# A fused attention and gated-MLP kernel: row tiles issued from two queues, a weight block moved to ScalarE's queue, and the second chunk's statistics moved behind gate work

## The chip, the cores and the metric

The kernel runs on one core of a Trainium2 chip. The metric is the device time of one execution in microseconds (us), the median over several runs. The span that the profile shows is about 1.8 us shorter than the device time of the same run. Each run also lists the mean clock that TensorE (PE) was granted. That turns out to matter here: a stretch of 3.41 us at half clock lowers the mean over 280 us by 0.006, so a run at 0.994 had about one such stretch and a run at 0.988 had two.

## The reference, cut to what matters

```python
xn = layernorm(x)                       # x: 2048 x 640, bf16
qkv = xn @ wqkv                         # 32 heads of 20
pq, pk = q @ w_phi, k @ w_phi           # per head
phi = concat(softmax(p), softmax(-p))   # for q and for k
o = (phi_q @ (phi_k^T v)) / (phi_q @ sum(phi_k))
mlp = (silu(xn @ w1) * (xn @ w3)) @ w2  # 640 -> 1536 -> 640
out = x + o @ wo + mlp
```

## The kernel before

The 2048 rows are worked in four chunks of 512 rows, each of four row tiles of 128. Chunk 0 is normalised tile by tile (statistics on VectorE, DVE; square root on ScalarE, ACT), turned by TensorE (PE) transposes and used at once. Chunks 1 to 3 go through DRAM and a DMA transpose. PE's order is fixed: transposes T(0), T(1), then V(0), T(2), V(1), T(3), V(2), V(3), three gate/up (GU) pairs, the matmuls that fold `w_phi` into the key weights ("prep") with two more pairs, then K(0). Each engine gets its instructions in one fixed order, and where it matters below it keeps to it (in the profile of after_fill DVE stands idle for 3.75 us at one instruction with ready work behind it). All loads are issued from SyncE's queue:

```python
def setup():
    ...
    for t in range(4):
        load_x(xg[0], t, 1, 0)              # row tiles of chunk 0, 160 KB each
    nc.sync.dma_start(out=wv[:], ...)       # 800 KB
    load_gu(0)                              # 1st gate/up block: w1 and w3, 480 KB each
    nc.sync.dma_start(out=wrow[:], ...)
    load_x(xg[1], 0, 4, 1)                  # rows of chunk 1, 640 KB
    nc.sync.dma_start_transpose(out=wkT[:], in_=A_wqkv[:, D : 2 * D])
    for i in range(1, 4):
        load_gu(i)
...
    for t in range(4, 8):
        ln_stats(t)                         # statistics of chunk 1: on DVE ahead of all gate work
...
LN(1)                                       # normalise chunk 1, store it, transpose it back
```

A GU pair needs two PSUM banks of six. ACT takes tanh of one (`th`), DVE multiplies (`gs`), ACT copies the other (`up`), and only then are the banks free.

The softmax here doesn't subtract the row's maximum and nothing guards it: scores larger than these inputs give would overflow.

Of the kernel before, what the change touches and what calls it, by code (L numbers as in the profile page):

```python
# [79 lines left out]
def kernel(  # L80
# [53 lines left out]
    xg = {}  # L134
# [17 lines left out]
    wqkv3 = A_wqkv.rearrange("(c p) f -> p c f", p=P)  # L152
    w13 = [w.rearrange("(c p) f -> p c f", p=P) for w in (B_w1, B_w3)]

    def load_x(dst, t0, n, k):
        nc.sync.dma_start(
            out=dst[:, t0 : t0 + n, :],
            in_=x2[512 * k + t0 * P : 512 * k + (t0 + n) * P, :].rearrange("(t p) d -> p t d", p=P),
        )

    def load_gu(i):
        for w, src in zip((w1, w3), w13):
            nc.sync.dma_start(out=w[:, :, 384 * i : 384 * i + 384], in_=src[:, :, 384 * i : 384 * i + 384])

    def setup():
        xg[0] = five.tile([P, 4, D], bf, name="xg", tag="five")
        xn[0] = five.tile([P, 4, D], bf, name="xn", tag="five")
        xg[1] = five.tile([P, 4, D], bf, name="xg", tag="five")
        for t in range(4):
            load_x(xg[0], t, 1, 0)  # L170
        nc.sync.dma_start(out=wv[:], in_=wqkv3[:, :, 2 * D : 3 * D])
        load_gu(0)
        nc.sync.dma_start(out=wrow[:], in_=A_w_phi.rearrange("h j f -> (h j) f").rearrange("(g p) f -> p g f", p=P))
        load_x(xg[1], 0, 4, 1)
        nc.sync.dma_start_transpose(out=wkT[:], in_=A_wqkv[:, D : 2 * D])
        for i in range(1, 4):
            load_gu(i)

    ident = consts.tile([P, P], bf, name="ident")
    eps = consts.tile([P, 1], f32, name="eps")  # L180
# [21 lines left out]
    def warm():  # L202
        nc.vector.memset(xnT[:, 0, 0:512], 0.0)
        ps = bank([P, 512], f32)
        for i in range(WARM):
            nc.tensor.matmul(ps[:], xnT[:, 0, 0:P], xnT[:, 0, 0:512])
# [35 lines left out]
                nc.gpsimd.tensor_copy(out=hi[:, :, HC - 1], in_=mask[64:128, 2 * g + 1, :])  # L242

    pinned = {}

    def order_after(ins, other):
        tc.add_manual_dep(
# [12 lines left out]
    def dve_us(n, x=1):  # L260
        return 0.065 + n / 960.0 / x
# [1 line left out]
    stats = consts.tile([P, NST, 2, nc.vector.BN_STATS_DIM], f32, name="stats")  # L263
    mv = consts.tile([P, NST, nc.vector.BN_AGGR_DIM], f32, name="mv")
    rstd = consts.tile([P, NST], f32, name="rstd")
    arrive = [3.0, 4.4, 5.8, 6.2] + [11.0] * 4 
    stats_of = {}
    apply_of = {}
    rstd_of = {}
# [7 lines left out]
    def ln_stats(t, k=None, parts=(0, 1)):  # L277
        c, i = divmod(t, 4)

        def fn():  # L280
            for h in parts:
                ins = nc.vector.bn_stats(out=stats[:, t, h, :], in_=xg[c][:, i, h * 320 : (h + 1) * 320])  # L282
                if k is not None:
                    order_after(ins, pinned[k])
            if parts[-1] == 1:
                nc.vector.bn_aggr(out=mv[:, t, :], in_=stats[:, t, :, :])

        stats_of[t] = plan.op(
            "DVE", 0.47 * len(parts), fn, after=arrive[t] if t < 8 else 0.0,
            deps=[X_of.get(t)] + (phik_of[k][:1] if k is not None else []),  # L290
        )
        return stats_of[t]

# [43 lines left out]
    def LN(c, k=None):  # L337
        ln_rstd(c)

        def al():  # L340
            xn[c] = five.tile([P, 4, D], bf, name="xn", tag="five")

        a = xn_of[c] = plan.alloc("five", al)
        ds = [ln_apply(4 * c + i, [a] + (phik_of[k][:1] if k is not None else []), k) for i in range(4)]
        st = plan.op(
            "SP", 0.5,
            lambda: nc.sync.dma_start(out=xn_d[c][:].rearrange("(t p) d -> p t d", p=P), in_=xn[c][:]),
            deps=ds, frees=[a], lat=3.5,
        )
        xt = plan.op(  # L350
            "SP", 0.5,
            lambda: nc.sync.dma_start_transpose(out=xnT[:, :, 512 * c : 512 * c + 512], in_=xn_d[c][:]),
            deps=[st], lat=5.0,
        )
        for t in range(4 * c, 4 * c + 4):
            XT_of[t] = xt
# [66 lines left out]
    def K(t):  # L423
# [52 lines left out]
            plan.op("POOL", 1.7, mul(1), deps=[r2, pkb], frees=[ekb]),  # L476
        ]

    def KV(t):
        def fn():  # L480
            for j in range(10):
                acc = (kva, kvb)[j % 2]
                nc.tensor.matmul(  # L483
                    acc[:, 84 * (j // 2) : 84 * (j // 2) + 84],
                    phik_b[t][:, j, :, :].rearrange("p a f -> p (a f)"),
                    vaug[t % 4][:, h0[j] : h0[j] + 4, :].rearrange("p h d -> p (h d)"),
                    start=(t == 0 and j < 2), stop=(t == NST - 1), skip_group_check=True,
                )

        KV_of[t] = plan.op("PE", pe_us(10, 90), fn, deps=phik_of[t] + V_of[t], frees=[phik_a[t]])  # L490
# [39 lines left out]
    def hT_alloc(c):  # L530
        def fn():
            hT[c] = hpool.tile([P, KF, 512], bf, name="hT", tag="hT")

        if c not in hT_a:
            hT_a[c] = plan.alloc("hT", fn)
        return hT_a[c]

    w13_at = [10.0, 18.5, 21.5, 24.5]

    def GU(c, fi, mode):  # L540
        xs = xnT[:, :, c * 512 : (c + 1) * 512]
        deps = [XT_of[4 * c + i] for i in range(4)]
        us = []
        for w in (w1, w3):
            o = {}

            def fn(o=o, w=w):
                o["ps"] = bank([P, 512], f32)
                for k in range(KD):
                    nc.tensor.matmul(  # L550
                        o["ps"][:], w[:, k, fi * P : (fi + 1) * P], xs[:, k, :], start=(k == 0), stop=(k == KD - 1)
                    )

            us.append((plan.op("PE", pe_us(KD, 512), fn, deps=deps, takes="bank", after=w13_at[fi // 3]), o))
        (ug, og), (uu, ou) = us
        box = {}

        ab = {}
        for n in ("th", "gs") if mode == "DVE" else ("th", "gs", "up"):
            def al(n=n):  # L560
                box[n] = work.tile([P, 512], bf, name=n, tag=n)

            ab[n] = plan.alloc(n, al)

        def th():
            nc.scalar.activation(out=box["th"][:], in_=og["ps"][:], func=AF.Tanh, scale=0.5)  # L566

        a = plan.op("ACT", act_us(512), th, deps=[ug, ab["th"]], frees=[ug])

        def gs():  # L570
            nc.vector.scalar_tensor_tensor(  # L571
                out=box["gs"][:], in0=box["th"][:], scalar=1.0, in1=og["ps"][:], op0=ALU.add, op1=ALU.mult
            )

        b = plan.op("DVE", dve_us(512), gs, deps=[a, ab["gs"]], frees=[ug, ab["th"]])
        hb = hT_alloc(c)
        if mode == "DVE":

            def hm():
                nc.vector.scalar_tensor_tensor(  # L580
                    out=hT[c][:, fi, :], in0=box["gs"][:], scalar=0.5, in1=ou["ps"][:], op0=ALU.mult, op1=ALU.mult
                )

            d = plan.op("DVE", dve_us(512), hm, deps=[b, uu, hb], frees=[uu, ab["gs"]])
        else:

            def uc():
                nc.scalar.activation(out=box["up"][:], in_=ou["ps"][:], func=AF.Copy, scale=0.5)  # L588

            e = plan.op("ACT", act_us(512), uc, deps=[uu, ab["up"]], frees=[uu])  # L590
            d = plan.op(
                "POOL", 1.3,
                lambda: nc.gpsimd.tensor_mul(out=hT[c][:, fi, :], in0=box["gs"][:], in1=box["up"][:]),  # L593
                deps=[b, e, hb], frees=[ab["gs"], ab["up"]],
            )
        GU_of.setdefault(c, []).append(d)
# [244 lines left out]
    ln_finish(2)  # L841
    ln_stats(3, parts=(1,))
    ln_sqrt(3)
    V(0)
    T(2, "DVE")
    V(1)
    ln_finish(3)
    T(3, "DVE")
    V(2)
    V(3)  # L850
    plan.op("ACT", 1.3, lambda: nc.scalar.preload_act_table(AF.Exp), deps=[rstd_of[3]])

    for t in range(4, 8):
        ln_stats(t)
    early = len(plan.ops)

    plan.op("SP", 0.5, lambda: nc.sync.dma_start_transpose(out=wqT[:], in_=A_wqkv[:, 0:D]), after=24.0)
    LN(1)
    plan.op("SP", 0.5, lambda: nc.sync.dma_start(out=w2[:], in_=B_w2.rearrange("(c p) d -> p c d", p=P)), after=36.0)

    def modes(n):
# [15 lines left out]
            owed = 0.0  # L877

    fill(3 * 2.16)
    for u in prep("k", wkT, wkphi, 13.0):  # L880
        u()
        fill(0.4)
    wq_seq = prep("q", wqT, wqphi, 34.0)
    for t in range(NST):
        K(t)
        if 1 <= t <= 8:
            fetch(7 + t, t)
        if t == 5 or t == 9:
            LN((t + 3) // 4, t)
        fill(1.95)  # L890
        if t >= 4:
            V(t)
        fill(1.95)
        if t >= 2:
            KV(t - 2)
        if 6 <= t < 11:
            for _ in range(2):
                wq_seq.pop(0)()
                fill(0.4)
# [46 lines left out]

    order = plan.run()
    with tc.manual_schedule(engines={ET.PE, ET.DVE, ET.Activation, ET.Pool, ET.SP}):
        warm()
        setup()  # L950
        constants()
        for o in plan.ops[:early]:
            o["fn"]()
# [35 lines left out]
```

## Time and profile before

| | before |
|---|---|
| median of the first 6 runs | 280.86 us |
| PE busy | 271.1 of 279.4 us |
| first V matmul, first gate/up matmul, K(0) | 8.92, 16.57, 29.49 us |

The head of the page of before (engine, busy us, share, instructions) says that PE is the limit:

```profile
span 279.4 us, 4902 instructions
PE 271.1 (97%) x1880; PEld 166.1 (59%) x1904; DVE 172.3 (62%) x284; ACT 147.1 (53%) x320; POOL 95.7 (34%) x124
```

PE's timeline of before, first 17 us (start, duration, engine, line, operation, what ended the idle time ahead). V (line 401) waits for `wv` and then runs at half speed: 10 matmuls take 2.01 and 2.49 us, while 20 take 2.88 us from 13.86 us on.

```profile
5.92 0.67 PE L379 MATMUL bank<-ident,xn 128*128 128x128 bf16 x5
7.03 0.45 PE L379 MATMUL bank<-ident,xn 128*128 128x128 bf16 x5 [0.43 <-DVE xn L327]
8.92 2.01 PE L401 MATMUL bank<-wv,xnT 128*128 128x320 bf16 x10 [1.44 <-DMA wv<-in_A_wqkv_dram]
11.26 2.49 PE L401 MATMUL bank<-wv,xnT 128*128 128x320 bf16 x10
13.86 2.88 PE L401 MATMUL bank<-wv,xnT 128*128 128x320 bf16 x20
16.57 1.24 PE L550 MATMUL bank<-xnT,w_99 128*128 128x512 bf16 x4
```

The windows view of before (window: length, busy us of PE, PEld, DVE, ACT, POOL, granted clock, DMA share, GB/s). The windows are cut where the clock records begin and end. In 6.38 to 9.80 us PE worked 1.54 of 3.42 us; the next 3.41 us ran at half clock.

```profile
6.38:9.80 3.42, 1.54 (x15) 1.03 (x14) 2.74 (x9) 1.86 (x5) 3.01 (x17) 1.00 1.08 351
9.80:13.21 3.41, 3.41 (x18) 2.17 (x17) 1.01 (x3) 1.23 (x3) 2.32 (x9) 0.50 1.28 260
```

The chain of waits of before (start, us, what), some pieces of its first 24 us.

```profile
2.65 6.23 DMA wv<-in_A_wqkv_dram
14.55 0.80 DVE stats L282 x2
17.57 0.76 DVE stats L282 x2
18.97 1.05 POOL rstd L298
20.05 0.80 DVE xn L327 x2
20.85 0.60 DVE gs L571
21.44 1.55 DVE xn L327 x2
22.99 0.61 DVE gs L571
23.64 0.32 PE bank L507 x3
```

### The profile page before, as it was taken

The numbers are of one execution on the slowest core, as the hardware profiler recorded it, in microseconds if no ns is written. First come the engines' busy times: TensorE is split into PE (matmuls) and PEld (weight loads), VectorE is DVE, ScalarE is ACT, GpSimd is POOL, SyncE is SP. The second block draws the span as 40 slices with busy tenths as digits, with TensorE's granted clock in tenths as the row PEclk, the third lists the DMA queues.
The fourth block names the chain that finished last, engine by engine and source line by source line (L and its number), as shares of the span: only waits on it lengthen the run. The fifth ranks groups of instructions, "written<-read, shape, count | busy, mean of one in ns | idle before, by whom it ended". The sixth has DMA issues, their size and how long they took to land.

```text
span 279.4 us, 4902 instructions
## 1 busy us (share of the span) xinstructions
PE 271.1 (97%) x1880; PEld 166.1 (59%) x1904; DVE 172.3 (62%) x284; ACT 147.1 (53%) x320; POOL 95.7 (34%) x124
## 2 busy tenths in 40 slices
PE   7799999999999999999999999999999999999995
PEld 3555555555566655557555577557665676457774
DVE  5475589979667974765439965732937229426421
ACT  3477776666667666667688723833228332532000
POOL 8716276675557453655312200001010110330000
PEclk9799999999999999999999999999999999999999
DMA  6999999002700060000300363361030621300311
GB/s 196 276 285 253 277 242 324 12 2 92 178 14 0 2 175 14 2 0 6 115 0 2 94 100 102 69 176 52 32 88 23 141 84 39 95 0 26 115 49 49
DMA packets 44103, 26.56 MB, mean 95 GB/s; under 512 B 26416, under 2 KB 44080, under 8 KB 44080
## 3 DMA queue, kind: packets, MB, share of 16 engines
q1 hardware_dynamic: 43936, 26.21, 35.3%
q8 instruction: 15, 0.25, 0.4%
q14 instruction: 8, 0.07, 0.1%
q10 hardware_dynamic: 144, 0.03, 0.1%
HBM read 12.81 MB, written 7.21 MB: 72 GB/s over the span
## 4 chain that ended last, share of the span: by engine, by line
PE 82%; DVE 7%; DMA 4%; ACT 2%; issue 2%; POOL 1%; SPq 1%; DVEq 0%; ACTq 0%
PE bank L550 31%; PE bank L793 18%; PE bank L401 13%; PE bank L797 8%; PE bank L637 6%; DMA wv<-in_A_wqkv_dram 2%; DVE xn L327 2%; PE bank L683 1%; PE rtbank L683 1%; DVE gs L571 1%; DMA oT<-od_91 1%; DVE stats L282 1%; PE kva L483 1%; PE bank L507 1%; PE kvb L483 1%
## 5 line engine op out<-in xcount | busy, mean ns | idle before, releaser
L593 POOL TENSOR_TENSOR hT<-gs,up 128x512 bf16<-128x512 bf16 x44 | 51.3, 1166 | 140.1 <-ACT up L588 87.4
L550 PE MATMUL bank<-xnT,w_99 128*128 128x512 bf16 x223 | 58.7, 379 | 1.1 <-DVE gs L571 0.2
L550 PE MATMUL bank<-xnT,w_100 128*128 128x512 bf16 x238 | 59.4, 379 | 0.1
L793 PE MATMUL bank<-w_101,hT 128*128 128x320 bf16 (+2 forms) x396 | 57.9, 295 | 0.0
L566 ACT ACTIVATE th<-bank 128x512 bf16<-128x512 f32 x48 | 29.1, 607 | 35.6 <-PE bank L550 35.5
L793 PEld LDWEIGHTS <-hT 128*128 128x128 bf16 x396 | 37.9, 98 | 14.6
L571 DVE SCALAR_TENSOR_TENSOR gs<-th,bank 128x512 bf16<-128x512 bf16 x48 | 32.5, 678 | 21.9 <-ACT th L566 21.9
L550 PEld LDWEIGHTS <-w_100 128*128 128x128 bf16 x240 | 23.5, 98 | 28.3
L401 PEld LDWEIGHTS <-xnT 128*128 128x128 bf16 x320 | 31.1, 100 | 15.1 <-issue 1.5
L802 DVE TENSOR_TENSOR res<-bank,xr 128x320 bf16<-128x320 f32 (+2 forms) x33 | 15.8, 480 | 36.2 <-PE bank L797 36.2
L588 ACT ACTIVATE up<-bank 128x512 bf16<-128x512 f32 x44 | 26.5, 603 | 21.7 <-PE bank L550 21.7
L550 PEld LDWEIGHTS <-w_99 128*128 128x128 bf16 x240 | 23.1, 98 | 22.1 <-issue 0.4
L449 DVE TENSOR_REDUCE ks<-ek 128x64 f32<-128x1280 bf16 x16 | 23.6, 1478 | 19.4 <-ACT ek L440 19.4
L466 POOL TENSOR_TENSOR phik<-ek,kr 128x640 bf16<-128x640 bf16 x16 | 29.8, 1861 | 6.7 <-PE bank L401 3.0
L797 PE MATMUL bank<-wo,oT 128*128 128x320 bf16 (+2 forms) x165 | 27.1, 295 | 0.2 <-DMA oT<-od_91 0.2
L401 PE MATMUL bank<-wv,xnT 128*128 128x320 bf16 x160 | 25.6, 311 | 1.4 <-DMA wv<-in_A_wqkv_dram 1.4
L440 ACT ACTIVATE ek<-bank 128x320 bf16<-128x320 f32 x64 | 23.1, 437 | 3.7 <-PE bank L401 3.5
L401 PE MATMUL bank<-wkphi,xnT 128*128 128x320 bf16 x160 | 24.3, 299 | 0.0
L637 PE MATMUL bank<-xnT,wqphi 128*128 128x512 bf16 x95 | 22.1, 379 | 0.3
L466 DVE TENSOR_TENSOR phik<-ek,kr 128x640 bf16<-128x640 bf16 x16 | 21.3, 1332 | 1.4
L797 PEld LDWEIGHTS <-oT 128*128 128x128 bf16 x165 | 15.8, 98 | 6.3 <-DMA oT<-od_91 0.5
L637 PEld LDWEIGHTS <-wqphi 128*128 128x128 bf16 x100 | 9.5, 98 | 10.4
(173 smaller groups left out, 256.4 us busy)
## 6 DMA issues: line engine op xcount, KB each, us to landing
xr<-in_A_x_dram SPq DMA_DIRECT2D x4, 640.0 KB, 5.0
out_dram<-res SPq DMA_DIRECT2D x15, 160.0 KB, 1.8
xg<-in_A_x_dram SPq DMA_DIRECT2D x12, 160.0 KB, 3.4
w_99<-in_B_w_dram SPq DMA_DIRECT2D x4, 480.0 KB, 7.7
w_100<-in_B_w_dram SPq DMA_DIRECT2D x4, 480.0 KB, 8.7
w_101<-in_B_w_dram SPq DMA_DIRECT2D x1, 1920.0 KB, 10.4
wv<-in_A_wqkv_dram SPq DMA_DIRECT2D x1, 800.0 KB, 6.2
wo<-in_A_wo_dram SPq DMA_DIRECT2D x1, 800.0 KB, 4.7
```

The lines of the kernel that those rows point to most:

```text
L401: nc.tensor.matmul(o["ps"][:], xnT[:, c, t * P : (t + 1) * P], w[:, c, 320 * half : 320 * half + 320], start=(c == 0), stop=(c == KD - 1),)
L440: nc.scalar.activation(out=box["ek"][:, sgn, 320 * half : 320 * half + 320], in_=o["ps"][:], func=AF.Exp, scale=1.0 - 2.0 * sgn,)
L449: nc.vector.reduce_sum(out=box["s"][:].rearrange("p a h -> p (a h)"), in_=box["ek"][:].rearrange("p a (h d) -> p (a h) d", d=Dh), axis=AX.X,)
L466: phik_ins[t] = eng.tensor_mul(out=phik_b[t][:, :, sgn, :], in0=box["ek"][:, sgn, :].rearrange("p (h d) -> p h d", d=Dh), in1=box["r"][:, ...
L550: nc.tensor.matmul(o["ps"][:], w[:, k, fi * P : (fi + 1) * P], xs[:, k, :], start=(k == 0), stop=(k == KD - 1))
L566: nc.scalar.activation(out=box["th"][:], in_=og["ps"][:], func=AF.Tanh, scale=0.5)
L571: nc.vector.scalar_tensor_tensor(out=box["gs"][:], in0=box["th"][:], scalar=1.0, in1=og["ps"][:], op0=ALU.add, op1=ALU.mult)
L588: nc.scalar.activation(out=box["up"][:], in_=ou["ps"][:], func=AF.Copy, scale=0.5)
L593: lambda: nc.gpsimd.tensor_mul(out=hT[c][:, fi, :], in0=box["gs"][:], in1=box["up"][:]),
L637: nc.tensor.matmul(o["ps"][:], wqphi[:, k, g * P : (g + 1) * P], xnT[:, k, c * 512 : (c + 1) * 512], start=(k == 0), stop=(k == KD - 1),)
L793: nc.tensor.matmul(o["ps"][:], hT[c][:, fi, ti * P : (ti + 1) * P], w2[:, fi, cols], start=(fi == 0), stop=False)
L797: nc.tensor.matmul(o["ps"][:], oT[c][:, k, ti * P : (ti + 1) * P], wo_of[0][:, k, cols], start=False, stop=(k == KD - 1))
```

## The change

Its intent is an earlier first V matmul (`wv` is issued after two row tiles instead of four), an earlier second gate/up block (no longer behind the transpose that keeps SyncE's queue busy for 6.4 us), and gate work on DVE that no longer stands behind chunk 1. Cut to its core (the rest only passes a queue or a pin through, and moves the numbers that the planner uses):

```diff
     def setup():
-        for t in range(4):
-            load_x(xg[0], t, 1, 0)
+        nc.vector.memset(xg[0][:, 2, 0:8], 0.0)
+        for t in range(0, 4, 2):
+            load_x(xg[0], t // 2, 1, 0)
+            load_x(xg[0], 2 + t // 2, 1, 0, nc.scalar)
         nc.sync.dma_start(out=wv[:], ...)
         load_gu(0)
         nc.sync.dma_start(out=wrow[:], ...)
-        load_x(xg[1], 0, 4, 1)
         nc.sync.dma_start_transpose(out=wkT[:], ...)
-        for i in range(1, 4):
-            load_gu(i)
+
+    def later():
+        load_x(xg[1], 0, 4, 1)
+        load_gu(2)
+        load_gu(3)
...
+    plan.op("ACT", 1.3, lambda: nc.scalar.preload_act_table(AF.Exp), ...)   # was behind V(3)
     V(0); T(2, "DVE"); V(1); ln_finish(3); T(3, "DVE")
+    plan.op("ACT", 0.5, lambda: load_gu(1, nc.scalar))
+    plan.op("SP", 0.5, later)
     V(2); V(3)
-    for t in range(4, 8):
-        ln_stats(t)
-    LN(1)
...
     fill(3 * 2.16)
+    for t in range(4, 8):
+        ln_stats(t, ("g", 0, t // 2 - 2))       # ordered behind gs 0 and gs 1
...
-        if t == 5 or t == 9:
-            LN((t + 3) // 4, t)
+        if t == 0 or t == 5 or t == 9:
+            LN((t + 3) // 4 if t else 1, t)     # LN(1) behind K(0)'s product on DVE
...
-        warm()
         setup()
+        warm()
```

More of the change, by code (lines that the diff above doesn't have):

```diff
@@ L153, with load_x @@
     w13 = [w.rearrange("(c p) f -> p c f", p=P) for w in (B_w1, B_w3)]
-    def load_x(dst, t0, n, k):
-        nc.sync.dma_start(
+    def load_x(dst, t0, n, k, queue=nc.sync):
+        queue.dma_start(
             out=dst[:, t0 : t0 + n, :],
@@ L159, in load_x, with load_gu @@
         )
-    def load_gu(i):
+    def load_gu(i, queue=nc.sync):
         for w, src in zip((w1, w3), w13):
-            nc.sync.dma_start(out=w[:, :, 384 * i : 384 * i + 384], in_=src[:, :, 384 * i : 384 * i + 384])
+            queue.dma_start(out=w[:, :, 384 * i : 384 * i + 384], in_=src[:, :, 384 * i : 384 * i + 384])
     def setup():
@@ L173, in setup @@
         nc.sync.dma_start(out=wrow[:], in_=A_w_phi.rearrange("h j f -> (h j) f").rearrange("(g p) f -> p g f", p=P))
+        nc.sync.dma_start_transpose(out=wkT[:], in_=A_wqkv[:, D : 2 * D])
+    def later():
         load_x(xg[1], 0, 4, 1)
-        nc.sync.dma_start_transpose(out=wkT[:], in_=A_wqkv[:, D : 2 * D])
-        for i in range(1, 4):
-            load_gu(i)
+        load_gu(2)
+        load_gu(3)
     ident = consts.tile([P, P], bf, name="ident")
@@ L244 @@
     pinned = {}
+    pin_of = {}
     def order_after(ins, other):
@@ L265 @@
     rstd = consts.tile([P, NST], f32, name="rstd")
-    arrive = [3.0, 4.4, 5.8, 6.2] + [11.0] * 4
+    arrive = [3.0, 3.4, 3.8, 4.2] + [15.0] * 4
     stats_of = {}
@@ L289, in ln_stats @@
             "DVE", 0.47 * len(parts), fn, after=arrive[t] if t < 8 else 0.0,
-            deps=[X_of.get(t)] + (phik_of[k][:1] if k is not None else []),
+            deps=[X_of.get(t), pin_of.get(k)],
         )
@@ L343, in LN @@
         a = xn_of[c] = plan.alloc("five", al)
-        ds = [ln_apply(4 * c + i, [a] + (phik_of[k][:1] if k is not None else []), k) for i in range(4)]
+        ds = [ln_apply(4 * c + i, [a, pin_of.get(k)], k) for i in range(4)]
         st = plan.op(
@@ L477, in K @@
         ]
+        pin_of[t] = phik_of[t][0]
     def KV(t):
@@ L536, in hT_alloc @@
         return hT_a[c]
-    w13_at = [10.0, 18.5, 21.5, 24.5]
+    w13_at = [10.0, 17.5, 22.5, 25.0]
     def GU(c, fi, mode):
@@ L570, in gs @@
         def gs():
-            nc.vector.scalar_tensor_tensor(
+            pinned["g", c, fi] = nc.vector.scalar_tensor_tensor(
                 out=box["gs"][:], in0=box["th"][:], scalar=1.0, in1=og["ps"][:], op0=ALU.add, op1=ALU.mult
@@ L575, in GU @@
         b = plan.op("DVE", dve_us(512), gs, deps=[a, ab["gs"]], frees=[ug, ab["th"]])
+        pin_of["g", c, fi] = b
         hb = hT_alloc(c)
@@ L843 @@
     ln_sqrt(3)
+    plan.op("ACT", 1.3, lambda: nc.scalar.preload_act_table(AF.Exp), deps=[rstd_of[3]])
     V(0)
@@ L848 @@
     T(3, "DVE")
-    V(2)
-    V(3)
-    plan.op("ACT", 1.3, lambda: nc.scalar.preload_act_table(AF.Exp), deps=[rstd_of[3]])
-    for t in range(4, 8):
-        ln_stats(t)
+    plan.op("ACT", 0.5, lambda: load_gu(1, nc.scalar))
+    plan.op("SP", 0.5, later)
+    V(2)
+    V(3)
     early = len(plan.ops)
     plan.op("SP", 0.5, lambda: nc.sync.dma_start_transpose(out=wqT[:], in_=A_wqkv[:, 0:D]), after=24.0)
-    LN(1)
     plan.op("SP", 0.5, lambda: nc.sync.dma_start(out=w2[:], in_=B_w2.rearrange("(c p) d -> p c d", p=P)), after=36.0)
@@ L948 @@
     with tc.manual_schedule(engines={ET.PE, ET.DVE, ET.Activation, ET.Pool, ET.SP}):
+        setup()
         warm()
-        setup()
         constants()
```

## The prediction

> **What bounds the kernel now.** TensorE. The page shows PE busy 271.1 of 279.4 us (97%); from 16.4 us on its waits are tiny (the longest is 0.3 us in the waits view). Only the first 16.4 us are worth winning. The PE timeline there: warm-up matmuls to 6.1 us; transposes of row tiles 0 and 1; a 1.44 us wait of the first V matmul for wv (to 8.92 us; chain of waits: "DMA wv 6.23", 2.2%); V of tiles 0 and 1 at about twice the normal time (10 matmuls in 2.0 and 2.5 us, against 20 in 2.9 us later), because the windows view grants clock 0.5 from about 9.9 to 13.3 us; gate/up starts at 16.44. The Trainium skill, "TensorE: Matmul & The Clock Gate" (Part 1), says a free-running window of about 3.4 us with little PE work throttles what follows; this trace agrees (3.4 us at 0.5 after the wait for wv).
>
> **What the change does.**
> 1. SyncE issues two row tiles instead of four before wv, at 0.41 to 0.43 us each (chain), so wv is issued near 1.7 instead of 2.65 us. The skill, "DMA: Bandwidth & Descriptors" (Issuing engines are not separate DMA queues), says two queues save only issue time; that counts here, as the DMA is under-used at first (windows: 142 GB/s in 0–5 us, 338 in 5–10). I estimate wv (1.47 MB with the rows) lands at 6.6–7.4 us, about when tile 0 is transposed and evicted (7.32 us).
> 2. V(0) starts near 7.4 us, 1.5 us earlier; PE stays busy enough that the half-clock window mostly goes: another 1.3–1.7 us. Given back: the DVE chain for tiles 2 and 3 (xn of tile 2 ends at 8.62 us anyway) and the Exp table load (1.28 us), now ahead of V's evictions, which makes V(2) wait for a bank, about 0.5 us. Gate/up should start at 14.1 (13.6–15.3): about 2.3 us gained.
> 3. The 6.38 us transpose issue on SyncE no longer delays the second gate/up block; ScalarE pays about 1.1 us of issue before V(2)'s evictions, hidden by the six banks. The block is needed at about 21.5 us and should land by 20: no stall, no gain.
> 4. Statistics and normalisation of chunk 1 (about 4.2 and 2.4 us of DVE) move behind gs and behind K(0)'s product, near 33–36 us. PE did not wait for them at 14–23 us: no direct gain. The risk: chunk 1's store and transpose (4.0 and 5.0 us to landing) end near 46 us, K(4) needs it near 48.6 us, and the load of w2 (10.4 us to landing) may now stand between them in SyncE's queue: 0 to 2 us of PE stall, one chance in three.
>
> After that everything is a shift: the same matmuls, in the same order, PE-bound.
>
> **Prediction.** 280.9 − 2.3 (head) + about 0.2 (risk in 4) gives 278.8 us, range 277.0 to 280.6. Chances: faster by over 2% 0.03, within 2% 0.95, slower 0.02.
>
> **What will show it.** Chain of waits: no DMA wv piece of 6 us. Timeline: first V matmul near 7.4 us, first gate/up near 14.1. Windows: clock 1.0 through 9–14 us. PE busy total down about 1.5–2 us. Waits of PE in 40–55 us near 0; if the risk comes true, a wait on the chunk 1 transpose.
>
> **What would make it wrong.** The clock window's phase may differ per execution, so V may still fall in a half-clock window (gain only about 1 us). Row tile 1 delayed by sharing with tiles 2 and 3. wv slowed by the other queue. The second gate/up block late because it shares bandwidth. DVE, 99% busy at 40–50 us already, falling behind with chunk 1's work.

## The result, and the profile after

| | before | after |
|---|---|---|
| median (40 and 20 runs) | 281.7 us | 281.1 us |
| lowest to highest | 279.91 to 283.76 | 278.95 to 286.02 |
| ratio of the fast runs | | 0.998 (0.9956 to 1.0003) |

Ratios are the mean time of one kernel's fast runs over that of the other's of the same rounds, so not quite the ratio of the quoted medians. The median lies outside the predicted range (277.0 to 280.6), and the gain, 0.6 us, is under a third of the 2.1 us expected. Yet the run that was profiled took 278.93 us, almost the predicted number, and its profile shows nearly every step as predicted. That agreement is the luck of one execution, as the runs below show. PE's timeline of after: V at 7.74 us at full speed, gate/up at 13.85 us.

```profile
span 277.2 us, 4904 instructions
PE 269.4 (97%) x1880; PEld 164.8 (59%) x1904; DVE 173.0 (62%) x285; ACT 146.6 (53%) x320; POOL 95.1 (34%) x124
```

```profile
7.45 0.45 PE L384 MATMUL bank<-ident,xn 128*128 128x128 bf16 x5 [0.85 <-DVE xn L332]
7.74 1.52 PE L406 MATMUL bank<-wv,xnT 128*128 128x320 bf16 x10
9.40 1.52 PE L406 MATMUL bank<-wv,xnT 128*128 128x320 bf16 x10
11.05 2.96 PE L406 MATMUL bank<-wv,xnT 128*128 128x320 bf16 x20
13.85 1.24 PE L557 MATMUL bank<-xnT,w_99 128*128 128x512 bf16 x4
```

The windows view of after: PE worked 2.56 of 3.42 us in the window that had 1.54 before, and no half clock follows.

```profile
6.36:9.78 3.42, 2.56 (x27) 1.82 (x25) 3.27 (x12) 1.83 (x5) 0.65 (x6) 1.00 1.16 301
9.78:13.19 3.41, 3.41 (x30) 2.36 (x28) 1.38 (x4) 3.38 (x8) 2.52 (x6) 1.00 1.20 232
```

The chain of after has no `wv` piece; its long early piece is the second gate/up block from ScalarE's queue, which landed 0.35 us after PE was ready for it.

```profile
11.77 10.57 DMA w_100<-in_B_w_dram
22.39 1.25 PE bank L557 x5
```

So the mechanism was there in this execution, and most of it was missing from the median. The two profiles also happen to stand at the same phase of the clock: the first stretch at full clock is recorded from 6.38 us in one and 6.36 us in the other (the 6.7 us of an expectation below is 0.3 us too late). The experiments ask what the other executions do.

### The profile page after: what moved, and what is told of

Same layout as the page of the kernel before. It is cut to its first block, busy times and chain, and to the rows that moved or that the text cites. A ratio compares the mean times of both kernels' runs of the same rounds, so it can differ in the third digit from the quotient of the medians.

```text
span 277.2 us, 4904 instructions
## 1 busy us (share of the span) xinstructions
PE 269.4 (97%) x1880; PEld 164.8 (59%) x1904; DVE 173.0 (62%) x285; ACT 146.6 (53%) x320; POOL 95.1 (34%) x124
## 4 chain that ended last, share of the span: by engine, by line
PE 80%; DMA 7%; DVE 7%; ACT 3%; issue 2%; SPq 0%; DVEq 0%; ACTq 0%
PE bank L557 31%; PE bank L801 18%; PE bank L406 12%; PE bank L805 8%; PE bank L645 6%; DMA w_100<-in_B_w_dram 4%; PE bank L691 1%; PE rtbank L691 1%; DVE xn L332 1%; DMA oT<-od_91 1%; DMA xg<-in_A_x_dram 1%; DVE phik L471 1%; PE kva L490 1%; PE kvb L490 1%; PE bank L514 1%
## 5 line engine op out<-in xcount | busy, mean ns | idle before, releaser
L406 PEld LDWEIGHTS <-xnT 128*128 128x128 bf16 x320 | 30.4, 98 | 13.0
L454 DVE TENSOR_REDUCE ks<-ek 128x64 f32<-128x1280 bf16 x16 | 23.6, 1476 | 16.9 <-ACT ek L445 16.9
L471 POOL TENSOR_TENSOR phik<-ek,kr 128x640 bf16<-128x640 bf16 x16 | 29.2, 1823 | 8.4 <-PE bank L406 3.0
L406 PE MATMUL bank<-wv,xnT 128*128 128x320 bf16 x160 | 24.3, 299 | 0.0
L471 DVE TENSOR_TENSOR phik<-ek,kr 128x640 bf16<-128x640 bf16 x16 | 22.1, 1384 | 1.7 <-PE bank L406 0.5
L287 DVE BATCH_NORM_STATS2 stats<-xg 128x6 f32<-128x320 bf16 x32 | 14.1, 473 | 2.8 <-DMA xg<-in_A_x_dram 2.8
```

The source lines that it names most:

```text
L406: nc.tensor.matmul(o["ps"][:], xnT[:, c, t * P : (t + 1) * P], w[:, c, 320 * half : 320 * half + 320], start=(c == 0), stop=(c == KD - 1),)
L454: nc.vector.reduce_sum(out=box["s"][:].rearrange("p a h -> p (a h)"), in_=box["ek"][:].rearrange("p a (h d) -> p (a h) d", d=Dh), axis=AX.X,)
L471: phik_ins[t] = eng.tensor_mul(out=phik_b[t][:, :, sgn, :], in0=box["ek"][:, sgn, :].rearrange("p (h d) -> p h d", d=Dh), in1=box["r"][:, ...
```

## The experiments

Five theories were tested. A: whether an execution suffers a half-clock stretch depends on the phase of the clock window, and the two profiles compared one phase. B, its rival: the gain is given back after the first 16 us. C: the rows of chunk 1 (SyncE's queue) and the second gate/up block (ScalarE's queue) race, and DVE, in order, waits for the loser. D, its rival: the spread at full clock has another cause. E: `w2` stands in front of chunk 1's store.

One table sums up the profiles, one execution each (all3_gu0late is told apart, below). "Rows" is when chunk 1's rows are issued and how long they take to land, "block" when the first half of the second gate/up block is issued from ScalarE. Apart from after_pin2_fill, the time is the start of K(0) plus 251.7 to 252.1 us: nearly everything that tells these kernels apart happens before K(0).

| profile | us | clock | V | GU | K(0) | rows: issue, to landing | block |
|---|---|---|---|---|---|---|---|
| before | 281.15 | 0.994 | 8.92 | 16.57 | 29.49 | 5.68, 8.3 | |
| before_again | 282.60 | 0.988 | 9.14 | 18.01 | 30.93 | 5.47, 8.7 | |
| before_fill | 281.11 | 1.000 | 9.31 | 15.29 | 29.29 | 5.23, 9.0 | |
| rows_only | 281.27 | 1.000 | 8.57 | 14.56 | 29.23 | 4.86, 8.8 | |
| after | 278.93 | 0.998 | 7.74 | 13.85 | 27.02 | 11.01, 5.8 | 11.34 |
| after_again | 281.26 | 0.994 | 8.33 | 16.47 | 29.12 | 12.28, 4.9 | 13.01 |
| after_third | 281.40 | 0.994 | 8.82 | 16.94 | 29.58 | 12.78, 4.7 | 13.30 |
| after_fill | 281.28 | 1.000 | 8.86 | 14.85 | 29.43 | 12.75, 8.4 | 12.06 |
| after_pin2 | 278.79 | 1.000 | 7.57 | 13.67 | 26.65 | 11.23, 6.2 | 11.17 |
| after_pin2_fill | 280.56 | 1.000 | 8.40 | 14.39 | 27.36 | 12.35, 8.4 | 11.60 |
| after_sync2 | 281.63 | 0.993 | 8.83 | 16.93 | 29.57 | 12.75, 4.6 | |
| after_w2late | 278.35 | 1.000 | 7.71 | 13.82 | 26.46 | 11.13, 6.5 | 11.31 |
| pin2_w2late | 278.56 | 0.999 | 7.76 | 13.75 | 26.72 | 11.84, 8.4 | 11.12 |
| all3 | 280.35 | 0.999 | 9.60 | 15.59 | 28.56 | 13.45, 8.4 | 12.80 |
| all3_again | 279.14 | 1.000 | 8.37 | 14.36 | 27.33 | 12.27, 8.4 | 11.57 |
| all3_wvfirst | 279.60 | 1.000 | 7.48 | 14.61 | 27.58 | 11.85, 5.9 | 12.10 |
| all3_halves | 278.33 | 1.000 | 7.59 | 13.70 | 26.67 | 12.34, 8.5 | 11.19 |

### Both kernels again, to read the clock of every run

Neither has an edit.

> The kernel before, unchanged, so that every run of it lists its granted clock. Theory A (clock window): about half of the change's expected gain came from removing a half-clock window of 3.4 us, and whether an execution has such a window depends on the phase of the clock window at its start; the two profiles happened to have the same phase (first full-clock record at 6.7 us). It expects the runs of before to split into a group at mean clock about 0.994 and a group at about 1.000, the second 1 to 2 us faster, spread 280 to 283.5 us. Theory B (the gain is given back after the first 16 us, by the second gate/up block's wait, by DVE or by the chunk 1 transpose): the clock explains less than 0.5 us of the spread.

> The kernel after, unchanged. Theory A: it splits by clock too, because its own idle time before 7.7 us still trips the window in some phases; runs at clock 1.000 lie 1.0 to 1.3 us below the runs of before at clock 1.000, runs at 0.994 as far below those of before at 0.994; the mean over all differs by less than 1 us. Theory B: at equal clock the two kernels differ by less than 0.3 us.

before_again came out at 0.9985 of before (0.9948 to 1.0022), as an unchanged kernel should; after_again at 1.0014 (0.9967 to 1.0061). Together with the runs of before in the later rounds and those of after in its first rounds and in after_third, all fast runs by clock are:

| fast runs | before: runs, mean us | after: runs, mean us |
|---|---|---|
| clock 0.998 or more | 11 of 50, 280.50 | 14 of 32, 280.17 |
| about 0.994 (0.991 to 0.997) | 26 of 50, 282.11 | 16 of 32, 281.95 |
| about 0.988 | 13 of 50, 283.05 | 2 of 32, 284.76 |
| all | 282.00 | 281.35 |

One run of after more (286.02 us, clock 0.982, so about three stretches) counts as slow by the 1.5% rule and is left out. Theory A holds for the split: an execution with one stretch is 1.6 to 1.8 us longer. But it was expected that at equal clock after would lie 1.0 to 1.3 us lower; it lies 0.16 to 0.33 us lower, and at 0.988 it is higher. That is near what theory B expected (less than 0.3 us). So A is half of the story, and within the full-clock group after spreads from 278.93 to 281.65 us, before only from 279.91 to 281.28: something else varies in after. (The groups are a selection: an execution whose V starts early seems less likely to lose its clock; of the three profiles of after, the one with V at 7.74 us kept it, those at 8.33 and 8.82 lost it. The table shows what goes together, not what a clock would be worth by itself: before_fill, below, keeps its clock in every run and takes 281.14 us, not 280.50.) With before's group means and after's shares the mean would be 281.46, so 0.54 of the 0.65 us between the two means goes with the shares of the groups (0.94 if after's means are taken with before's shares, where two runs at 0.988 weigh much).

The windows of after_again around its half clock: PE worked 1.75 of 3.42 us, and the following stretch is at half clock, with V in it. The first full-clock record stands at 4.56 us here, at 6.36 us in the profile of after.

```profile
4.56:7.98 3.42, 1.75 (x14) 0.82 (x13) 3.03 (x10) 1.17 (x3) 2.31 (x17) 1.00 0.97 313
7.98:11.39 3.41, 3.09 (x16) 1.91 (x15) 1.74 (x6) 2.41 (x4) 0.00 (x0) 0.50 1.22 224
```

### Idle matmuls in PE's gaps

```diff
+    def idle_fill(count, cols):             # PE only; zeros; kva's bank is not in use yet
+        ... nc.tensor.matmul(kva[:, 0:cols], spare[:, 0:P], spare[:, 0:cols]) ...
     T(0, "ACT")
+    idle_fill(2, 256)        # before_fill; after_fill: idle_fill(5, 256) and WARM = 12
     ...
     T(1, "ACT")
+    idle_fill(10, 256)       # before_fill only
```

> Before, with idle matmuls of zeros put into PE's two gaps ahead of the first V matmul (2 of 256 columns after the transpose of tile 0, 10 after that of tile 1), all else in the same order. Theory A: nearly all runs at clock 0.998 or more, spread under 1.5 us, mean 1 to 1.5 us below before (about 280.4). Theory B: within 0.3 us of before.

> After, with one more warm-up matmul and 5 idle matmuls of 256 columns after the transpose of tile 0. Theory A: nearly all runs at clock 0.998 or more, mean about 279.3, about 1.1 us below before_fill and 1.5 to 2 us below after. Theory B: within 0.3 us of after.

The half clock is gone: all 12 runs are at 0.999 or more. before_fill takes 281.14 us on average (0.996, 0.9935 to 0.9986), within 280.75 to 281.42; after_fill takes 280.61 (0.9941, 0.99 to 0.9983), from 277.98 to 282.01. Against before of the same rounds (282.24 us on average) before_fill gains 1.1 us, as theory A expected (1 to 1.5), though not down to the 280.4 named; so keeping the clock is worth about that in before. after_fill lies 2.05 us below after_again, but only 0.53 below before_fill where 1.1 was expected, and it did not become narrow. The profiles say why. before_fill starts gate/up 1.28 us earlier than before (15.29 against 16.57) and K(0) only 0.2 us earlier: PE's timeline has a wait in prep that was not there.

```profile
15.29 6.64 PE L559 MATMUL bank<-xnT,w 128*128 128x512 bf16 x29
21.77 0.48 PE L516 MATMUL bank<-wphi,wkT 128*128 128x140 bf16 x6
23.44 0.32 PE L516 MATMUL bank<-wphi,wkT 128*128 128x140 bf16 x3 [1.19 <-DVE gs L580]
```

The DVE work on chunk 1, which follows its rows' landing and not PE, holds `gs` and with it the banks. It was as late as PE in before, so an earlier PE only runs into it. In after_fill the same wait (1.8 us) has another cause. Its DVE timeline, then the landings (size, us from issue to landing):

```profile
16.75 0.69 DVE L587 SCALAR_TENSOR_TENSOR gs<-th,bank 128x512 bf16<-128x512 bf16 x1 [3.93 <-ACT th L582]
21.20 1.28 DVE L296 BATCH_NORM_STATS2 stats<-xg 128x6 f32<-128x320 bf16 x3 [3.75 <-DMA xg<-in_A_x_dram]
22.86 0.67 DVE L587 SCALAR_TENSOR_TENSOR gs<-th,bank 128x512 bf16<-128x512 bf16 x1
```

```profile
w<-in_B_w_dram ACTq DMA_DIRECT2D x2, 480.0 KB, 4.9
xg<-in_A_x_dram SPq DMA_DIRECT2D x1, 640.0 KB, 8.4
```

In after the rows landed in 5.8 us and the block's two halves in 6.4 and 10.6:

```profile
xg<-in_A_x_dram SPq DMA_DIRECT2D x1, 640.0 KB, 5.8
w_99<-in_B_w_dram ACTq DMA_DIRECT2D x1, 480.0 KB, 6.4
w_100<-in_B_w_dram ACTq DMA_DIRECT2D x1, 480.0 KB, 10.6
```

The Trainium skill, "DMA: Bandwidth & Descriptors" (Issuing engines are not separate DMA queues), says that transfers from several queues run on the same 16 engines and interleave. They share the engines here too, but not evenly. Of the twelve profiles in the table with the block on ScalarE's queue, the rows land within 6.5 us in the six where they are issued before the block or within 0.1 us of it, and in 8.4 to 8.5 us in the six where the block is 0.65 us or more ahead (five of these have idle matmuls; pin2_w2late has none). Which happens depends on when SyncE starts to issue the `wkT` transpose just before, on how long that takes (6.48 us in after, 8.63 us in after_fill) and on when ACT gets to the block. This is theory C: the statistics are pinned behind `gs` 0 but still stand ahead of `gs` 1, so when the rows lose, DVE waits 3.75 us for them with `gs` 1 behind it, and PE waits for a bank.

### The statistics pinned later; the block back on SyncE; the row tiles alone

```diff
-        ln_stats(t, ("g", 0, t // 2 - 2))
+        ln_stats(t, ("g", 0, 2))            # after_pin2; after_pin2_fill adds the idle matmuls
```

```diff
-    plan.op("ACT", 0.5, lambda: load_gu(1, nc.scalar))     # after_sync2
     def later():
         load_x(xg[1], 0, 4, 1)
+        load_gu(1)
```

rows_only is before with only the four added lines at the top of `setup()` and the swap of `warm()` and `setup()`.

> After, with one edit: all four statistics of chunk 1 are pinned behind the gs of gate/up block 2 instead of 0 and 1. Theory C: in after, the rows of chunk 1 (SyncE) and the second gate/up block (ScalarE) race for the same DMA engines; where the rows lose, DVE, in order, waits for them ahead of the second gs (landing 21.2 instead of 16.9 us in the profile of after_fill) and PE loses 1.8 us on a bank. With the pin later this wait is off PE's path: no PE wait for gs over 0.5 us before 30 us. The clock lottery stays. Mean 0.5 to 1 us below after (about 280.5), runs at clock 1.000 within 278 to 279.5. Theory D (the spread at clock 1.000 has another cause): same spread of 3 us at clock 1.000 and same mean as after.

> The later pin and the idle matmuls together. Theories A and C together: both losses gone, all runs at clock 0.998 or more, mean about 278.3, spread under 1.5 us. Theory D: as after_fill, 278 to 282.

> After, with the second gate/up block issued from SyncE again, directly behind the rows of chunk 1; nothing on ScalarE's queue after the row tiles. Theory C: the rows always land first, by 17.5 us; runs at clock 1.000 within 278 to 279.7, mean as after_pin2 or up to 0.5 us above (the block may land just after 21 us). Theory D: as after.

> Before, with only the row tiles alternated between the two queues (and issued ahead of the warm-up). wv should land by 7.5 us and V start near 7.7 us as in after, gate/up near 13.9 where the clock stays full; but chunk 1's statistics and normalisation stand ahead of gs as in before, so DVE (bound by the chunk 1 rows' landing, about 13.5 us, plus 6.5 us of work) makes PE wait 1 to 2 us for a bank near 20 to 22 us. Theory: at most 0.7 us below before; the rival, that an early V is worth its 1.2 us alone, says 1.2 or more.

rows_only came out at 0.9992 (0.995 to 1.0034): nothing, as expected, though gate/up starts at 14.56 us in its profile. PE then waits 1.8 us for `gs`, and K(0) starts at 29.23, as late as in before_fill. An earlier V alone shows no gain here, though the interval would hide one of the size that after has.

after_pin2 came out at 0.9911 (0.9874 to 0.9947) with five fast runs that all happened to be at clock 1.000, from 278.62 to 280.30 us; the sixth (284.31 us, clock 0.988) counts as slow, and the ratio flatters the kernel for it. Three of the five lie above the 278 to 279.5 expected. after_pin2_fill, 279.42 to 280.96 us, all at 0.999 or more, came out at 0.9935 (0.9903 to 0.9966). No profile with the later pin has a wait for `gs` of more than 0.2 us, also not those five where the rows lost the race (after_pin2_fill, pin2_w2late, all3, all3_again, all3_halves): theory C's mechanism is shown, and from V to K(0) after_pin2_fill takes 18.96 us against 20.57 in after_fill. The runs bear it out in their spread: at clock 0.998 or more the kernels with the early pin and the block on ScalarE's queue reach 281.65 (after), 282.01 (after_fill) and 281.66 us (after_w2late, below), and no run with the later pin passes 280.96. In the means it does not show by itself: after_fill is 0.9941 of before, after_pin2_fill 0.9935. And in all three profiles of after the rows were issued first, so how many of its own executions lose the race is not known. after_sync2 (0.9963, 0.9927 to 0.9998) fits it too, as the rows land in 4.6 us and there is no `gs` wait, but its profile is at half clock, where after_again and after_third show no `gs` wait either; four of its six runs lost the clock, and its mean (281.02) is above the range expected. So it decides little. At clock 1.000 it took 279.37 and 280.72; the second is 1 us above the expected range.

after_pin2_fill missed its 278.3, and its profile names a further loss, the risk that the prediction's point 4 had put at one in three. PE waits 1.1 us, until 49.9 us, for the transpose of chunk 1 (waits view of after_pin2_fill: who waited for whom, us in total, times, longest):

```profile
PE bank L415 <- DMA xnT<-xnd: 1.1, 1, 1.1
```

SyncE's queue in that profile's timeline: `w2` (`w`, 1.9 MB) is issued at 31.35, ahead of the store (`xnd`) at 37.05; the transpose can be issued only when the store has landed, at 45.11.

```profile
31.35 0.43 SPq L875 DMA_DIRECT2D w<-in_B_w_dram  x1
37.05 0.40 SPq L361 DMA_DIRECT2D xnd<-xn  x1
45.11 2.63 SPq L366 DMA_TRANSPOSE xnT<-xnd  x1
```

In after the store took 6.5 us to land, against 4.0 in before, and the transpose, issued at 43.20 and landing 4.7 us later (47.9), was 0.4 us ahead of the matmul that needs it (48.32).

### `w2` issued behind the transpose

```diff
-    plan.op("SP", 0.5, lambda: nc.sync.dma_start(out=w2[:], ...), after=36.0)
+    def load_w2():
+        order_after(nc.sync.dma_start(out=w2[:], ...), pinned["xnT", 1])   # planned after LN(1)
```

pin2_w2late adds the later pin, all3 the pin and the idle matmuls.

> After, with one edit: w2 (1.9 MB, not used before 157 us) is issued behind chunk 1's transpose on SyncE instead of ahead of its store. Theory E: in after, w2's bytes stand before the store (6.5 us to landing against 4.0 in before), so the transpose lands 0.4 us before K(4) needs it in the good execution and after it in others (PE wait 1.1 us in the profile of after_pin2_fill). It expects the store to land in 3 to 4 us, the transpose near 44 us, no PE wait on the transpose in any execution, and a mean 0.2 to 0.6 us below after_third. Rival: the wait was an accident of that execution, no difference.

> Later pin of the statistics and late w2, no idle matmuls. Theories A, C, E: the half-clock lottery alone is left; runs at clock 1.000 at 277.5 to 279.3, runs at 0.994 about 1.7 to 2 us above them; mean about 279.5.

> Idle matmuls, later pin, late w2. Theories A, C, E together: every run at clock 0.998 or more, 277.3 to 279.3, the rest of the spread coming from the landing of wv (V starting between 7.6 and 8.9 us); mean about 278.3, 3 to 3.7 us below before. If a fourth loss is there, the mean stays above 279.5.

> The kernel after once more, on the same chip and in the same rounds as the three above, for the comparison with them. Mean 280.5 to 281.8, two groups by clock.

In SyncE's timeline of after_w2late the store is issued at 36.15 and the transpose already at 39.66 us, 3.5 us later against 8.1 in after_pin2_fill, so theory E's mechanism is shown:

```profile
36.15 0.40 SPq L355 DMA_DIRECT2D xnd<-xn  x1
39.66 2.69 SPq L351 DMA_TRANSPOSE xnT<-xnd  x1
42.40 0.57 SPq L868 DMA_DIRECT2D w<-in_B_w_dram  x1
```

What it is worth by itself is not: after_w2late came out at 0.9918 (0.9857 to 0.9978) by four fast runs, and its other two (283.25 and 283.34 us, clock 0.992 and 0.994) were left out as slow, so that all six average 281.06 against 281.61 for the six of after_third. That PE waits for this transpose was seen in one profile only. after_third came out at 0.9978 (0.993 to 1.0027), with four of six runs at 0.994. pin2_w2late came out at 0.9919 (0.9871 to 0.9967), with four runs at full clock within 278.56 to 279.62 and two at 0.994 at 281.63 and 281.85: they split by clock, but by 2.6 us, more than the 1.7 to 2 expected, so something else (a late `wv`, perhaps) goes with it. all3 came out at 0.9894 (0.9855 to 0.9933), six runs within 278.52 to 280.35 and all at 0.999 or more; its mean, 279.27, is 1 us above what was expected. Its profile is one of the worse executions: V starts at 9.60 us, after 2.0 us of waiting for `wv`.

### What holds `wv` back

In the twelve profiles that load row tiles and `wv` as after does (rows_only to all3_again in the table, with after), V starts between 7.57 and 9.60 us, median 8.4; `wv` lands 5.3 to 7.8 us after its issue at 1.7 us. The prediction had said 7.4 for V.

```diff
-        load_gu(0)                                             # all3_gu0late: from ACT, after T(0)
+    plan.op("ACT", 0.0, lambda: load_gu(0, nc.scalar))
```

```diff
-        nc.sync.dma_start(out=wv[:], ...)                      # all3_halves
+        for h in range(2):
+            nc.sync.dma_start(out=wv[:, :, 320 * h : 320 * h + 320], ...)
```

all3_wvfirst issues row tile 0 and then `wv` from SyncE, and tiles 1 to 3 from ScalarE. all3_again is all3.

> all3 with the first gate/up block (0.98 MB) taken from behind wv and issued from ScalarE near 7 us. Theory F (wv's last packets are late because engines that have finished their part of wv go on with the gate/up block and take bandwidth from those that have not): the tail goes, V starts at 7.2 to 7.7 us, mean of the runs 0.3 to 0.7 us below all3_again, unless the block then lands after 13.7 us and PE waits for it. Rival (a few of the 16 engines are late whatever stands behind): V start as before, 7.6 to 9.6.

> all3 with wv issued second on SyncE, after row tile 0 alone; tiles 1 to 3 from ScalarE. Theory G (wv is late because of what is ahead of it): wv issued 0.4 us earlier lands at least as much earlier, V at 7.2 to 8.5 us; tile 1 may come later and stretch the DVE chain by up to 0.5 us. Mean between all3_again minus 0.5 and plus 0.5.

> all3 with wv in two transfers by column halves (640-byte runs instead of 1280). V's first half needs only the first: V starts at 7.2 to 7.6 in nearly every execution, the second half waits up to 1 us. [...] Mean 0 to 0.4 us below all3_again.

> all3 unchanged: all runs at clock 0.998 or more, mean 279.0 to 279.6, as in its first time (279.27), V start anywhere from 7.5 to 9.6 us.

all3_halves is the best version: 278.17 to 278.82 us in six runs, mean 278.54, 0.9895 of before (0.9856 to 0.9934), and 0.63 us below all3_again (279.17; 0.9916 of before, 0.9879 to 0.9953), where 0 to 0.4 was expected. V starts at 7.59 us in its profile: it needs only the first half, which landed 4.5 us after its issue, and the second (6.2 us) is not waited for. all3_wvfirst (0.9925, 0.9887 to 0.9963) moved V to 7.48 us, but T(2) then waited 0.86 us for its normalised tile, and its mean (279.43) is that of all3_again within noise.

all3_gu0late failed as an experiment: 290.06 us (median), 1.0298 of before. ACT did no other work for 8.92 us before and during the issue of the second gate/up block, with V's evictions behind it, and PE waited 6.0 us for a bank; SyncE's order had also changed. V started at 7.75 us, but that happens with the block in its place too. What delays `wv` in some executions stays open. The line of the waits view of all3_gu0late:

```profile
PE bank L567 <- ACT vaug L429: 6.0, 1, 6.0
```

## Why the prediction was wrong

- **What bounds it.** PE busy was read correctly, but "from 16.4 us on its waits are tiny ... Only the first 16.4 us are worth winning" was the first false step. PE did not wait because it was late itself. (This alone did not cost the change its gain, as the change moves that work as well.) The chain of before ran over DVE's chunk 1 work until 23.6 us, and when PE alone was made earlier (before_fill by 1.28 us, rows_only by 2.01 us at gate/up) K(0) moved by 0.20 and 0.26 us.
- **Point 1, wv "lands at 6.6–7.4 us".** The mechanism was right and the term mis-sized: `wv` landed at 7.0 to 9.5 us. V starts at a median of 8.4 us in the twelve profiles, against 8.92 to 9.31 in the three of before: some 0.75 us gained (9.14 − 8.39), not 1.5.
- **Point 2, "the half-clock window mostly goes: another 1.3–1.7 us".** This step failed. It went in the profiled execution. Over the fast runs, 78% of before's and 56% of after's have such a stretch (this is the step "PE stays busy enough": in after_again PE worked 1.75 of 3.42 us ahead of it). By the shares of the groups some 0.5 us of the term came in. The prediction named the phase as a risk and gave it no weight. The Trainium skill, "TensorE: Matmul & The Clock Gate" (Part 1), says the window is free-running and its phase differs between runs of one kernel, and the profiles agree: the first full-clock record stands anywhere from 4.12 to 7.03 us in the eighteen.
- **Point 3, "no stall, no gain".** Failed. The block was needed and issued about when foreseen, but in 0.65 us or more of lead over chunk 1's rows it delays them from 5.8 to 8.4 us; that costs 1.8 us of PE in the profile of after_fill, through DVE. In the three profiles of after itself it did not happen, so what it takes from the median of after is inferred from the spread at full clock and not measured.
- **Point 4, "no direct gain".** Failed in its sign: moving the chunk 1 work is what lets the earlier start through at all (K(0) at 27.02 in after, 29.23 in rows_only). Its risk was real in kind and size: 1.1 us in one profile, a margin of 0.4 us in that of after.
- **The sum.** 278.8 us is about what a good execution takes (278.93). The mean of the executions needs things at once that vary from run to run, the clock, the race, the transpose behind `w2` and the landing of `wv`, and after leaves them to chance. all3_halves takes the first three away and makes V need only half of `wv`, and lies at 278.54 us, so the size of the predicted gain was there to be had, though not from this change. How the loss in after splits between the four stays open. Also, before was taken as 280.86 us from six runs; 40 runs put it at 281.7.

## What to carry to other kernels

Before costing an earlier start, ask for each engine when it could have been ready, not whether it waited: two chains that arrive together hide each other's waits, and only moving both pays. When the expected gain is under 1%, take the clock and the spread of every run first; one profile is one draw, and two profiles at the same phase can show an effect that the median does not have. A statistic pinned behind one piece of work is still in front of the next, so on an engine that keeps its order pin anything that waits for a DMA behind all the work that must not wait.

## What the Trainium skill lacked or had wrong

- "DMA: Bandwidth & Descriptors" (Issuing engines are not separate DMA queues) says that issuing from several engines only saves issue time and that the transfers interleave. Neither it nor the page's paragraph on arbitration between queues says what the order of issue across two queues does to the landing: here 640 KB on SyncE's queue took 8.4 to 8.5 us to land when 960 KB on ScalarE's queue had been issued 0.65 us or more earlier (six profiles), and 4.7 to 6.5 us otherwise (six profiles of kernels with the block on ScalarE's queue).
- "TensorE: Matmul & The Clock Gate" (Part 1) calls the ramp under 1% of a typical span and advises against fitting it. The size agrees (1.6 to 1.8 us of 281 for one stretch), but where a change is worth as little it decides the result. For the fall to half clock the page names a whole idle window (about 3.4 us). It lacks how busy PE must be in a window to keep its clock: in the first 10 us here, full-clock windows with 1.39 to 1.75 us of PE work (before, before_again, after_again, after_third, after_sync2) were followed by half clock, and those with 1.79 us (after_w2late) or more were not. Busy time alone does not fix the bound: windows with 1.58 us (rows_only) and 1.64 us (after_fill) around 22 us kept the clock.
- No page gives the time for which a DMA transpose of this size out of DRAM holds its issuing queue: the issue of `wkT` (800 KB) took SyncE 6.27 to 8.63 us in the profiles of after and of kernels made from it, all3_gu0late (5.31) aside, and that variation is one of the things that decided the race above.
- No page gives how far the landing of one load varies between executions: `wv` (800 KB), issued at 1.7 us each time, took 5.3 to 7.8 us in the twelve profiles (V from 7.57 to 9.60 us); the cause is open.
